# Seven places instead of five for rounded operands, and five steps ahead instead of three, in two of four matrix products

## The chip, the cores and the metric

The kernel runs on one core of one Trainium2 chip. The metric is the device time of one execution in microseconds (us), lower is better. TensorE (PE, with its weight loads PEld) multiplies, VectorE (DVE) and ScalarE (ACT) work element by element, GpSimd (POOL) does little here, and SyncE (SP) issues nearly all DMAs from one queue, in order. Each engine runs its own instructions in the order in which they stand in the program, and waits for the others by semaphores.

## The reference, cut to what matters

An attention with 32 memory slots per head, and behind it two feed-forward blocks:

```
x = attention(q, k, v, phi)            # 4608 tokens x 512
g = relu(x @ w_in1) ** 2               # 512 -> 2048
y = g @ w_out1                         # 2048 -> 512
g = silu(y @ w_in2)                    # 512 -> 2048
out = g @ w_out2                       # 2048 -> 512
```

## The kernel before, in words

There are four matrix products in a row. The first (attention and w_in1) fills the time up to about 337 us. The function `second` computes the second product (w_out1, 337 to 700 us) and, called once more, the last one (w_out2, from about 1049 us to the end). The third product (w_in2) lies between them.

**What `second` does.** The tokens are cut into 6 batches of 768. A batch is computed by a seven-product scheme for 2x2 blocks: instead of eight block products there are seven, named after their right-hand operands B11, B21, T2, T1, T3, B22, T4 (`PRODUCTS`), in this order. B11 to B22 are the loaded blocks (tiles `r`, from `g` in memory), T1 to T4 are sums of them that DVE makes in place (T1 = B12 - B11, T2 = B22 - T1, T3 = B22 - B12, T4 = B21 - T2; lines 758 to 767). In the second product only, ACT first squares each loaded block (line 746).

**A step.** Each of the seven products is done in four steps, one for each quarter h of the inner dimension, so a batch has 28 steps and `second` 168. For a step two things must be ready: its weights (`ws`, on chip), and its operand in two parts, a rounded one and the rest: ACT rounds the operand into the first half of a tile `c` (line 770), and DVE writes what the rounding lost into the second half (line 771). PE then does 12 matmuls of 128x128 by 128x384 (line 799): for each of two weight tiles and two output halves rounded times rounded, rounded times rest, rest times rounded. The first of each three needs only ACT's half, the second needs DVE's.

**What `combos` issues.** One call makes the operand of one step: the squares (for the first step of each pair of blocks), the sums, and the two halves of `c`. The calls run ahead of PE by `AHEAD` steps in the program:

```
for k in range(AHEAD):
    ahead(k)
for k, (b, n, h) in enumerate(steps):
    ahead(k + AHEAD)
```

At the first step of a batch `ahead` also issues the 16 loads of that batch's blocks. A load waits until DVE no longer needs what lies in its place.

**The places.** The tiles `c` come from the pool `s` under the tag "g", which has a fixed number of places. A new `c` needs a place whose former tile has been read for the last time: for another `c` that is PE's last matmul on it. The third product uses the same tag for its output tiles (`g2t`, two for each pair of weight tiles), which leave their place when their DMA to memory has landed. The pools of `second` lie on chip where those of the first product lay.

**What sets the order.** The program is written step by step, but a scheduler then orders each engine's instructions by an estimate of its own of when each can run. The order in which the code emits them decides between those that are ready.

Of the kernel before, what the change touches and what calls it, by code (L numbers as in the profile page):

```python
# [76 lines left out]
def attention_moe_moe(ctx: ExitStack, tc, q, kv, phi, w_in1, w_out1, w_in2, w_out2, out):  # L77
# [577 lines left out]

    pools = [tc.tile_pool(name=n, bufs=k, reuse_waits="tile") for n, k in (("wk", 1), ("wl", 1), ("xa", 1), ("xb", 1), ("s", 5), ("u", 2))]
    wk, wl, xa, xb, spool, upool = (ctx.enter_context(p) for p in pools)
    psum = ctx.enter_context(tc.tile_pool(name="ps", bufs=1, space=PSUM, reuse_waits="tile"))  # L660
    W.update({q: (wk if q < WR + 2 else wl).tile([P, SLOTS, 2, 2 * P], F32R, tag=f"w{q}", name=f"ws{q}") for q in range(WR, NQ)})
# [40 lines left out]
    QS = 2  # L702
    NH = NQ // QS
    HQ = NQ // 2
    AHEAD = 3

    NAMES = ("B11", "B21", "B12", "B22", "T2")
    FREED = ("B11", "T2", "B12", "B22", "B21")
# [4 lines left out]
    def second(src, order, square, to, weights, begin, tiles=tuple(range(10))):  # L713
# [61 lines left out]
        def ahead(k):  # L775
            if k < len(steps):
                b, n, h = steps[k]
                if n == h == 0 and b:
                    quarters(b)
                combos(b, n, h)  # L780

        start = len(begun)
        begin(quarters)
# [4 lines that stand above are left out]
            bank = PRODUCTS[n][1]  # L788
# [221 lines left out]
```

## Time and profile before

| | |
|---|---|
| median of 3 runs | 1420.09 us (1415.77 to 1420.38) |
| the profiled execution | 1416.34 us |
| its span, first to last instruction | 1414.6 us |
| PE busy | 1375.0 us, 97% |
| PEld, DVE, ACT busy | 1311.8, 965.9, 790.7 us |
| DMA queue of SP | 386.62 MB, 80.4% of 16 engines |

The profile is one execution. "Busy" is the time in which an engine executes; what stands behind "<-" names whoever ended a wait. PE's matmuls overlap, so that one takes some 335 ns while the next starts about 174 ns after it. How many start in a stretch is therefore the better measure of PE's pace.

### The profile page before, as it was taken

The numbers are of one execution on the slowest core, as the hardware profiler recorded it, in microseconds if no ns is written. First come the engines' busy times: TensorE is split into PE (matmuls) and PEld (weight loads), VectorE is DVE, ScalarE is ACT, GpSimd is POOL, SyncE is SP. The second block draws the span as 40 slices with busy tenths as digits, with TensorE's granted clock in tenths as the row PEclk, the third lists the DMA queues.
The fourth block names the chain that finished last, engine by engine and source line by source line (L and its number), as shares of the span: only waits on it lengthen the run. The fifth ranks groups of instructions, "written<-read, shape, count | busy, mean of one in ns | idle before, by whom it ended". The sixth has DMA issues, their size and how long they took to land.

```text
span 1414.6 us, 25254 instructions
## 1 busy us (share of the span) xinstructions
PE 1375.0 (97%) x9266; PEld 1311.8 (93%) x9266; DVE 965.9 (68%) x1578; ACT 790.7 (56%) x1305; POOL 22.3 (2%) x44
## 2 busy tenths in 40 slices
PE   6999999999999999999999999999999999999999
PEld 4777877889899999999999999999998999999998
DVE  4666766764697878879756656565438858678583
ACT  3656666676668677685546455454434444444443
POOL 0000000000000000000000000000000000000000
PEclk9999999999999999999999999999999999999999
DMA  9979999899778878789997877879998576665750
GB/s 316 338 250 325 320 335 302 270 340 385 229 240 301 272 265 293 241 296 317 371 312 250 317 274 263 310 251 308 364 400 304 160 244 196 215 218 162 236 153 34
DMA packets 208444, 388.24 MB, mean 274 GB/s; under 512 B 19264, under 2 KB 90944, under 8 KB 208320
## 3 DMA queue, kind: packets, MB, share of 16 engines
q1 hardware_dynamic: 208320, 386.62, 80.4%
q8 instruction: 73, 1.20, 0.3%
q14 instruction: 51, 0.42, 0.1%
HBM read 253.38 MB, written 133.17 MB: 273 GB/s over the span
## 4 chain that ended last, share of the span: by engine, by line
PE 61%; DMA 5%; DVE 3%; ACT 1%; issue 1%; SPq 0%; DVEq 0%; ACTq 0%
PE psa L799 22%; PE psa L918 13%; PE psc L799 12%; PE psc L918 6%; PE psb L799 4%; PE psb L918 3%; DMA r<-g 2%; DVE c L771 1%; DMA ws<-w2o 1%; DMA g<-g2t 1%; DMA st<-moe_w_in 1%; ACT c L770 1%; ACT r L746 1%; DVE r L764 0%; DVE r L767 0%
## 5 line engine op out<-in xcount | busy, mean ns | idle before, releaser
L771 DVE TENSOR_TENSOR c<-r,c 128x768 fp32r<-128x768 f32 x336 | 318.1, 956 | 171.4 <-ACT c L770 171.1
L799 PE MATMUL psa<-c,ws 128*128 128x384 f32 x2304 | 416.0, 337 | 9.9 <-DVE c L771 6.1
L799 PEld LDWEIGHTS psa<-c,ws 128*128 128x128 f32 x2304 | 403.4, 189 | 13.8 <-DVE c L771 8.8
L770 ACT CAST c<-r 128x768 fp32r<-128x768 f32 x336 | 278.4, 835 | 222.9 <-PE psa L799 112.4
L918 PE MATMUL psa<-xc,ws 128*128 128x384 f32 x1152 | 218.0, 336 | 0.0
L613 PEld LDWEIGHTS h<-at,wp 128*128 128x128 f32 x1344 | 180.6, 188 | 36.4 <-ACT gt L622 21.4
L799 PE MATMUL psc<-c,ws 128*128 128x384 f32 x1152 | 206.5, 335 | 2.8 <-ACT c L770 2.8
L799 PEld LDWEIGHTS psc<-c,ws 128*128 128x128 f32 x1152 | 201.0, 188 | 3.2 <-ACT c L770 3.2
L613 PE MATMUL h<-at,wp 128*128 128x288 f32 x1344 | 196.2, 300 | 7.1 <-ACT gt L622 7.1
L918 PEld LDWEIGHTS psa<-xc,ws 128*128 128x128 f32 x1152 | 202.4, 188 | 0.0
L918 PE MATMUL psc<-xc,ws 128*128 128x384 f32 x576 | 110.9, 335 | 0.0
L799 PE MATMUL psb<-c,ws 128*128 128x384 f32 x576 | 106.3, 339 | 1.0 <-DVE c L771 1.0
L799 PEld LDWEIGHTS psb<-c,ws 128*128 128x128 f32 x576 | 101.3, 189 | 2.5 <-DVE c L771 2.4
L918 PEld LDWEIGHTS psc<-xc,ws 128*128 128x128 f32 x576 | 101.2, 188 | 0.0
L622 ACT ACTIVATE gt<-h 128x576 f32<-128x576 f32 x112 | 72.2, 648 | 42.5 <-PE h L613 38.4
L746 ACT ACTIVATE r<-r 128x768 f32<-128x768 f32 x96 | 80.0, 845 | 28.0 <-DMA r<-g 26.3
L206 DVE TENSOR_TENSOR pp<-pw,pp 128x256 f32<-128x256 f32 x148 | 61.3, 420 | 50.0 <-ACT pp L205 48.5
L205 ACT CAST pp<-pw 128x256 fp32r<-128x256 f32 x148 | 58.7, 403 | 55.4 <-DMA w2o<-pp 24.1
L162 ACT CAST top<-st 128x256 f16<-128x256 bf16 (+1 forms) x112 | 57.8, 527 | 31.0 <-DMA st<-moe_w_out 16.7
L932 ACT ACTIVATE g2t<-g2t 128x1152 f32<-128x1152 f32 x48 | 55.1, 1165 | 28.9 <-DVE g2t L683 28.7
L166 DVE SCALAR_TENSOR_TENSOR pw<-st,top 128x256 int32<-128x256 int32 x96 | 41.0, 430 | 36.4 <-ACT top L162 35.4
L685 ACT COPY u<-psa 128x384 f32<-128x384 f32 x72 | 33.9, 475 | 48.0 <-PE psa L918 20.4
(99 smaller groups left out, 1174.6 us busy)
## 6 DMA issues: line engine op xcount, KB each, us to landing
r<-g SPq DMA_DIRECT2D x192, 384.0 KB, 5.0
g<-g2t SPq DMA_DIRECT2D x48, 768.0 KB, 7.1
ws<-w2i SPq DMA_DIRECT2D x136, 256.0 KB, 5.2
ws<-w2o SPq DMA_DIRECT2D x136, 256.0 KB, 3.5
ws<-w1o SPq DMA_DIRECT2D x116, 256.0 KB, 4.5
g<-gt SPq DMA_DIRECT2D x64, 384.0 KB, 5.6
kv<-kv SPq DMA_DIRECT2D x32, 516.0 KB, 6.4
st<-moe_w_out SPq DMA_DIRECT2D x64, 256.0 KB, 5.1
```

The lines of the kernel that those rows point to most:

```text
L162: ins = nc.scalar.copy(top.bitcast(F16).rearrange("p (n h) -> p n h", h=2)[:, :, 1], flat.bitcast(BF16).rearrange("p (n h) -> p n h", h=4) ...
L166: to_f32.last = nc.vector.scalar_tensor_tensor(f.bitcast(I32), flat.rearrange("p (n w) -> p n w", w=2)[:, :n, 1], 13, top, op0=ALU.logical ...
L205: held(nc.scalar.copy(hi, w[:, of]))
L206: tt(lo, w[:, of], hi.bitcast(F32), op=ALU.subtract)
L613: mm = nc.tensor.matmul(h[:, half, :HALF], wp[b, j][:, g, s, fo:fo + P], attnT[b][:, x, g, tk], start=(k == 0), stop=(k == len(ops) - 1),)
L622: nc.scalar.activation(gt[:, f % 2].rearrange("p (h t) -> p h t", h=2), h[:, :, :HALF], AF.Relu)
L746: nc.scalar.activation(raw[b, name, h], raw[b, name, h], AF.Square)
L770: nc.scalar.copy(c[:, 0], r(name))
L771: tt(c[:, 1], r(name), c[:, 0].bitcast(F32), op=ALU.subtract)
L799: mm = nc.tensor.matmul(ps[o][bank], W[h * QS + u][:, slot(n), wi, o * P:(o + 1) * P], x[:, xi, u], start=(n in FIRST and h == u == m == 0 ...
L918: mm = nc.tensor.matmul(ps[q][bank], W[q][:, slot(n), wi, k * P:(k + 1) * P], x[:, xi, k], start=(n in FIRST and k == 0 and m == 0), stop= ...
L932: nc.scalar.activation(gq[q][:, :3], gq[q][:, :3], AF.Silu)
```

## The change

The pool of the rounded operands gets seven places instead of five, and `second` issues the operands five steps ahead instead of three. Nothing is added or removed: DVE has 1578 instructions in both programs, ACT 1305, and SP issues 1204 DMAs.

```diff
-    pools = [tc.tile_pool(name=n, bufs=k, reuse_waits="tile") for n, k in (("wk", 1), ("wl", 1), ("xa", 1), ("xb", 1), ("s", 5), ("u", 2))]
+    pools = [tc.tile_pool(name=n, bufs=k, reuse_waits="tile") for n, k in (("wk", 1), ("wl", 1), ("xa", 1), ("xb", 1), ("s", 7), ("u", 2))]
...
-    AHEAD = 3
+    AHEAD = 5
```

Since both numbers go into the scheduler, the order on the engines changes. On DVE in the second product, second batch, these rows stood from the rest of B21's first quarter (c_4965) to that of its fourth (c_5020); r_5040 and r_5041 are T2, and pp belongs to the preparation of the next weights:

```order
L771 TENSOR_TENSOR c_4965<-r_4863,c_4965 128x768
L758 TENSOR_TENSOR r_4858<-r_4870,r_4858 128x768
L771 TENSOR_TENSOR c_4982<-r_4863,c_4982 128x768
L762 TENSOR_TENSOR r_5041<-r_4876,r_4858 128x768
L764 TENSOR_TENSOR r_4870<-r_4876,r_4870 128x768
L771 TENSOR_TENSOR c_4999<-r_4864,c_4999 128x768
L206 TENSOR_TENSOR pp_7600<-pw_7555,pp_7600 128x256
L206 TENSOR_TENSOR pp_7604<-pw_7555,pp_7604 128x256
L767 TENSOR_TENSOR r_4863<-r_4863,r_5040 128x768
L762 TENSOR_TENSOR r_5041<-r_4876,r_4858 128x768
L771 TENSOR_TENSOR c_5020<-r_4864,c_5020 128x768
```

Now the same four (c_4931 to c_4992) stand as follows; T2 is r_5008 and r_5009:

```order
L771 TENSOR_TENSOR c_4931<-r_4833,c_4931 128x768
L758 TENSOR_TENSOR r_4828<-r_4840,r_4828 128x768
L215 TENSOR_TENSOR pw_7555<-pw_7555 128x256
L758 TENSOR_TENSOR r_4828<-r_4840,r_4828 128x768
L771 TENSOR_TENSOR c_4956<-r_4833,c_4956 128x768
L767 TENSOR_TENSOR r_4833<-r_4833,r_5008 128x768
L771 TENSOR_TENSOR c_4975<-r_4834,c_4975 128x768
L762 TENSOR_TENSOR r_5009<-r_4846,r_4828 128x768
L764 TENSOR_TENSOR r_4840<-r_4846,r_4840 128x768
L216 TENSOR_TENSOR pw_7555<-pw_7555 128x256
L771 TENSOR_TENSOR c_4992<-r_4834,c_4992 128x768
```

The four have moved ahead of work that isn't theirs: from the last rest of the batch before (T4, fourth quarter) to that of B21's fourth quarter DVE had 31 instructions, 20 of them of 128x768, and has 26 now, 19 of them of 128x768.

On ACT, where the third product ends and the last one begins, these rows stood (c_11525 to c_11534 are the four quarters of B11, c_11551 and c_11566 the first two of B21; g2t is the third product's output):

```order
L770 CAST c_11525<-r_11453 128x768
L932 ACTIVATE g2t_10935<-g2t_10935 128x1152
L932 ACTIVATE g2t_10936<-g2t_10936 128x1152
L770 CAST c_11528<-r_11453 128x768
L934 ACTIVATE g2t_10935<-psa_10937 128x384
L770 CAST c_11531<-r_11454 128x768
L770 CAST c_11534<-r_11454 128x768
L770 CAST c_11551<-r_11459 128x768
L770 CAST c_11566<-r_11459 128x768
```

Now there are (c_11537, c_11540 and c_11557 are the first three quarters of B21):

```order
L770 CAST c_11525<-r_11453 128x768
L690 COPY u2_10985<-psa_10937 128x384
L770 CAST c_11528<-r_11453 128x768
L690 COPY u2_10987<-psa_10944 128x384
L770 CAST c_11531<-r_11454 128x768
L932 ACTIVATE g2t_10935<-g2t_10935 128x1152
L932 ACTIVATE g2t_10936<-g2t_10936 128x1152
L770 CAST c_11534<-r_11454 128x768
L770 CAST c_11537<-r_11459 128x768
L770 CAST c_11540<-r_11459 128x768
L770 CAST c_11557<-r_11460 128x768
L934 ACTIVATE g2t_10935<-psa_10937 128x384
L685 COPY u1_11606<-psa_11543 128x384
```

Three roundings now stand ahead of the third product's last activations, where there was one. Behind this piece, and behind a copy of PE's sums of B11 (u1, L685), comes the rounding of B21's fourth quarter. On DVE its rest and T2's first quarter stand there now, at the start of the last product, as follows (c_11572 and c_11591):

```order
L771 TENSOR_TENSOR c_11572<-r_11460,c_11572 128x768
L758 TENSOR_TENSOR r_11453<-r_11489,r_11453 128x768 x2
L758 TENSOR_TENSOR r_11454<-r_11490,r_11454 128x768 x2
L762 TENSOR_TENSOR r_11588<-r_11495,r_11453 128x768
L764 TENSOR_TENSOR r_11489<-r_11495,r_11489 128x768
L767 TENSOR_TENSOR r_11459<-r_11459,r_11588 128x768
L762 TENSOR_TENSOR r_11588<-r_11495,r_11453 128x768
L764 TENSOR_TENSOR r_11489<-r_11495,r_11489 128x768
L771 TENSOR_TENSOR c_11591<-r_11588,c_11591 128x768
```

All the sums of T1 stand behind B21's last rest now; before, they were mixed in between the rests of B21, and 5 instructions stood between the last of these and T2's first. At the start of the second product nothing has moved: DVE's first 38 instructions there stand in the same order in both programs.

## Rows read from the trace of the kernel before

**Rows 1.** The page's first part: busy time, share of the span, instructions.
```profile
PE 1375.0 (97%) x9266; PEld 1311.8 (93%) x9266; DVE 965.9 (68%) x1578; ACT 790.7 (56%) x1305; POOL 22.3 (2%) x44
```

**Rows 2.** Stretches of the span: busy time and instructions by engine, clock, DMA.
```profile
337.00:400.00 63.00, 59.02 (x325) 57.66 (x326) 46.40 (x61) 46.28 (x68) 0.00 (x0) 0.97 0.79 266
400.00:460.00 60.00, 58.70 (x334) 57.86 (x333) 51.65 (x75) 42.52 (x69) 0.00 (x0) 1.00 0.83 280
460.00:520.00 60.00, 60.00 (x347) 60.00 (x346) 48.41 (x72) 43.43 (x70) 0.00 (x0) 1.00 0.79 263
520.00:580.00 60.00, 58.79 (x333) 57.49 (x332) 51.26 (x75) 41.80 (x68) 0.00 (x0) 1.00 0.85 282
...
640.00:700.00 60.00, 59.35 (x341) 59.03 (x340) 54.38 (x78) 33.14 (x53) 0.00 (x0) 1.00 0.97 343
700.00:1049.00 349.00, 349.00 (x2004) 349.00 (x2004) 197.03 (x369) 174.94 (x317) 0.00 (x0) 1.00 0.87 303
1049.00:1080.00 31.00, 25.55 (x131) 23.95 (x131) 22.59 (x28) 13.02 (x18) 0.00 (x0) 0.94 0.93 350
1080.00:1414.00 334.00, 331.07 (x1901) 330.75 (x1900) 232.71 (x275) 150.21 (x202) 0.00 (x0) 1.00 0.58 186
```

**Rows 3.** PE's waits, 400 to 700 us: total, times, longest.
```profile
PE psa L799 <- DVE c L771: 2.1, 3, 0.9
PE psb L799 <- DVE c L771: 1.0, 2, 0.7
```

**Rows 4.** Waits of all engines, 364 to 396 us.
```profile
DVE c L771 <- ACT c L770: 14.2, 11, 3.3
ACT r L746 <- DMA r<-g: 7.3, 6, 3.9
```

**Rows 5.** Stretches in the second product's first and second batch, columns as in rows 2.
```profile
346.00:366.00 20.00, 16.73 (x85) 15.70 (x84) 19.73 (x25) 11.55 (x17) 0.00 (x0) 0.91 0.70 237
366.00:396.00 30.00, 30.00 (x175) 30.00 (x174) 15.84 (x22) 25.69 (x40) 0.00 (x0) 1.00 0.82 258
396.00:421.00 25.00, 23.73 (x134) 22.90 (x132) 25.00 (x37) 14.02 (x24) 0.00 (x0) 1.00 0.72 236
```

**Rows 6.** Groups of instructions by line: busy us, mean ns, then idle before.
```profile
L770 ACT CAST c<-r 128x768 fp32r<-128x768 f32 x336 | 278.4, 835 | 222.9 <-PE psa L799 112.4 <-PE psc L799 49.7 <-PE psb L799 39.2
L746 ACT ACTIVATE r<-r 128x768 f32<-128x768 f32 x96 | 80.0, 845 | 28.0 <-DMA r<-g 26.3 <-DVE pw L166 0.8 <-DVE pp L206 0.4
```

**Rows 7.** PE's waits, 1040 to 1090 us.
```profile
PE psa L799 <- DVE c L771: 3.2, 2, 2.8
PE psa L799 <- ACT c L770: 2.3, 3, 1.0
```

**Rows 8.** ACT in order of time, 1041 to 1062 us: start, length, instruction, wait.
```profile
1056.01 1.56 ACT L770 CAST c<-r 128x768 fp32r<-128x768 f32 x2 [1.25 <-PE psa L799]
...
1059.94 1.57 ACT L770 CAST c<-r 128x768 fp32r<-128x768 f32 x2 [2.37 <-PE psa L799]
```

**Rows 9.** PE in order of time, 1047 to 1086 us.
```profile
1049.34 2.27 PE L799 MATMUL psa<-c,ws 128*128 128x384 f32 x12
...
1073.12 3.11 PE L799 MATMUL psa<-c,ws 128*128 128x384 f32 x12 [2.79 <-DVE c L771]
...
1085.22 1.04 PE L799 MATMUL psc<-c,ws 128*128 128x384 f32 x5
```

**Rows 10.** DVE in order of time, 1044 to 1082 us.
```profile
1072.11 0.95 DVE L771 TENSOR_TENSOR c<-r,c 128x768 fp32r<-128x768 f32 x1
...
1079.93 1.82 DVE L771 TENSOR_TENSOR c<-r,c 128x768 fp32r<-128x768 f32 x2
```

**Rows 11.** The stretch behind PE's longest wait there, columns as in rows 2.
```profile
1074.50:1077.90 3.40, 3.40 (x12) 3.40 (x11) 3.40 (x5) 1.29 (x2) 0.00 (x0) 0.50 0.22 33
```

**Rows 12.** ACT and DVE in order of time, around 393 to 400 us.
```profile
393.28 0.85 ACT L746 ACTIVATE r<-r 128x768 f32<-128x768 f32 x1 [0.34 <-DMA r<-g]
...
399.77 0.95 DVE L758 TENSOR_TENSOR r<-r 128x768 f32<-128x768 f32 x1
```

## The prediction

> **What bounds the kernel now.** I read the page's first part first: PE is busy 97% of the span, no other engine above 68% [rows 1]. So only stretches in which PE falls short can give time back. The windows show them [rows 2]. I take counts of matmuls rather than busy time, since a busy PE need not be at its pace. In 460 to 520 us PE never stops and does 347 matmuls in 60 us (0.173 us each), in the third product 2004 in 349 us (0.174). I take 0.1735 us, or 346 in 60 us; a step of 12 is 2.08 us. By this pace the losses are:
>
> - 337 to 400 us: 325 instead of 363, 38 x 0.1735 = 6.6 us (first batch of the second product).
> - 400 to 460, 520 to 580 and 640 to 700 us: 334, 333 and 341 instead of 346, 30 x 0.1735 = 5.2 us. Each holds a batch's passage from B21 to T2.
> - 1049 to 1080 us: 131 instead of 179, 48 x 0.1735 = 8.3 us (start of the last product).
> - 460 to 520 us, the third product and the last product's rest: nothing that can be told from the pace.
>
> Together 20.1 us. Who ends the waits: after 400 us DVE with the rests [rows 3]; at the last product's start DVE with the rests (3.2 us, one wait of 2.8) and ACT with the roundings (2.3 us) [rows 7].
>
> **Why PE waits at T2.** In 366 to 396 us DVE is busy 15.84 of 30 us, then 25.00 of 25 us in 396 to 421 [rows 5]: first it waits 14.2 us for roundings [rows 4], then the sums for T2 and T1 come at once and it runs late. What it lacks is a lead, worked up while it idled. The lead is limited by places: ACT's roundings wait longest for PE, 222.9, 112.4 and 39.2 + 49.7 us by PE's three banks [rows 6].
>
> **Stage one of the change, the second product's later batches.** Two more places and two more steps let the operands stand two steps further ahead, 2 x 2.08 = 4.2 us. The largest single loss is 13 x 0.1735 = 2.3 us. Besides, DVE's order changes: from the old batch's last rest to B21's last rest there are 26 instructions instead of 31, one less of 128x768. One of those starts 0.87 us after the other (0.95 long, 1.82 for two) [rows 10], so work that is not this batch's is put behind it. I take all of the 5.2 us as gone. Bounds: with the pace of 347 per 60 us the loss is 33 x 0.173 = 5.7 us; PE's plain waits for DVE are only 2.1 + 1.0 = 3.1 us [rows 3]. So 3.1 to 5.7.
>
> **Stage two, the last product's start.** Four of the five places hold the third product's outputs, so the first roundings pass through the fifth one after another: ACT waits 1.25 and 2.37 us for PE's matmuls on the rounding before [rows 8], and PE waits in its turn. With seven places three are free, and three roundings stand ahead of the old activations in ACT's order. From 1049.34 us PE does 96 matmuls up to T2 (12 of them the third product's), in the order of both programs, and 54 up to the end of B11. Unstalled, B11 ends at 1049.34 + 54 x 0.1735 = 1058.7 and T2 is reached at 1066.0 us; its first two matmuls (0.6 us with their tail) need no rest, so from 1066.6 on PE waits. Before it waited from 1073.12 - 2.79 = 1070.3 on [rows 9], 3.7 us later.
>
> But then comes the next wait. In the new ACT order the rounding of B21's last quarter stands behind two copies of B11's sums (0.48 each), so it ends at about 1059.7, and its rest on DVE at 1060.6. Behind that stand nine sums and T2's rest, ten times 0.87 = 8.7: T2's rest is ready at 1069.3. Before it was ready at 1072.11 + 0.95 = 1073.06 [rows 10], 3.8 us later. So PE waits 2.7 us, as long as before (2.8). What follows is paced by DVE with the same instructions, some in another order; the passage that PE reached at 1085.22 [rows 9] I expect at 1081.8: a gain of 3.4 us.
>
> PE's clock belongs to this. In the 3.4 us behind the long wait the granted clock is 0.50, the 1.2 GHz level, and PE does 12 matmuls where its pace gives 19.6: 7.6 x 0.1735 = 1.3 us [rows 11]. As the wait stays, I leave this loss in; if it goes too, the gain is 4.7. If the T2 wait grows by all that is won before it, the gain is 0. So 0 to 4.7, and 3.4 taken. The Trainium skill, "TensorE: Matmul & The Clock Gate", Part 1, says that the throttled state is the default and activity releases it; by this rule a T2 wait that shrank would give the 1.3 us back too (-9.9 instead of -8.6 in the sum below), and the trace agrees in so far as the drop stands behind the wait.
>
> **What I cost at nothing.** The first batch of the second product: DVE is busy 19.73 of 20 us in 346 to 366 [rows 5] and its first 38 instructions stand in the same order, so 6.6 us stay. The third product has no loss [rows 2], so more places for its outputs give nothing. The last product behind 1080 us likewise. The pool is 12 KB per partition larger and lies over the first product's places: between 0 and one wait for a transfer, longest 3.9 us [rows 4]; I take 0. The 16 loads of a batch are issued two steps earlier in the program on SP; they still wait for DVE's last use of their place, and the weights queued behind them are used some 12 steps later (25 us, the cover): 0, or again 3.9 once if that cover were gone.
>
> **The sum.** -5.2 - 3.4 = -8.6 us. The profiled execution took 1416.34 us (span 1414.6 and 1.7 around it), so 1407.7, a factor of 0.9939. The median of the runs is 3.75 us above the profiled one; the same factor gives 1420.09 x 0.9939 = 1411.5 us.
>
> **Rivals.**
>
> 1. *The lead in the second product is not set by places.* Then the change doesn't do there what it says. For it: in 364 to 396 us no wait of ACT for PE is among the long ones; ACT waits 7.3 us for loads before its squares [rows 4] and is busy 25.69 of 30 us [rows 5]. Squares and roundings in ACT's order may set the lead. Against it: the roundings now stand earlier in that order. Only stage two's gain: 1416.34 - 3.4 = 1412.9, median 1416.7.
> 2. *The T2 wait eats the gain at the last product.* For it: the chain of DVE there has no gap. Only the 5.2: 1411.1, median 1414.9.
> 3. *All waits are lack of space.* With it all 20.1 us would go: 1396.2, median 1400. Against it stands the first batch, where DVE itself has no time left [rows 5]. The Trainium skill, "Perfetto Trace Analysis", section "Identifying Performance Opportunities", says that a gap that repeats on the engine that should be saturated can mean too little memory for the next tile; by this rule the same would follow. The trace bears it out at the last product's start alone.
> 4. *Nothing that can be measured:* both stages find other limits, 1420.
> 5. *Slower: squares come late.* ACT is 86% busy in 366 to 396 us [rows 5], and two more roundings (2 x 0.835 us [rows 6]) stand ahead of squares. The last square starts at 393.28 and ends at 394.13; the first sum that needs it starts at 399.77 [rows 12], a margin of 5.6 us. Beyond this, the sum waits, and as DVE is in order all rests queued behind it, then PE. Two roundings take 1.7 us of the margin, so it holds unless loads add 3.9 us. To be slower by over 0.3% it must cost 8.6 + 4.3 = 12.9 us in five batches, 2.6 each: squares 8.2 us later than now.
>
> **How the numbers follow.** About 0.3%, or 4.3 us, is what a measurement of this kernel can tell from no change. Both stages as summed 0.60 (likeliest range 3.1 + 3.4 to 5.7 + 4.7, median 1409.7 to 1413.6); rival 1 0.15; rival 2 0.10; rival 3 0.03; rival 4 0.07; rival 5 0.05. Faster by over 0.3% (below 1415.8): the sum, rival 3, over half of rival 2, a fifth of rival 1, 0.71. Slower: 0.06. Else 0.23. The prediction is 1411.5 us, that of the likeliest case. The range goes from 1405 (a gain of both stages at its bound, and the runs' own spread of over 4 us) to 1418 (rival 1 with a little added); what lies outside is rival 3, 4 for the most part, and 5.
>
> **What the new profile would show.** Right: 345 to 347 matmuls in 400 to 460, 520 to 580 and 640 to 700 us, shifted a little, and no waits of PE for DVE there; at the last product's start no wait of ACT or PE for each other up to T2, T2's rest near 1069 us less what was won before it, a wait of about 2.7 us there, and the clock at 0.50 behind it; the first batch as it was, with 6.6 us lost. Wrong: PE still waits for rests at T2 in the second, fourth and sixth batch (then the lead isn't the places'); DVE waits for squares there (rival 5); or the T2 wait of the last product is 5 us or more (rival 2).

## The result, and the profile after

With the change the kernel takes 1407.07 us (median of 6 runs, 1405.54 to 1411.67), before 1420.24 us (6 runs): a ratio of 0.9919, 95% interval 0.9901 to 0.9937. The forecast was 1411.5 us. Timed once more beside other kernels it took 1410.12 us, 0.9944 (0.9924 to 0.9963). The two intervals overlap, and the ratio that the forecast used, 0.9939, lies in the second and just above the first.

The profiled execution took 1405.59 us with a span of 1403.8. These are its stretches, to be held against [rows 2] (columns: window; then length, busy time and instructions of PE, PEld, DVE, ACT, POOL; granted clock; DMA share; GB/s):

```profile
337.00:400.00 63.00, 59.90 (x333) 59.25 (x334) 48.95 (x63) 47.31 (x70) 0.00 (x0) 0.97 0.78 267
400.00:460.00 60.00, 60.00 (x346) 60.00 (x345) 52.79 (x77) 44.43 (x72) 0.00 (x0) 1.00 0.81 279
460.00:520.00 60.00, 60.00 (x347) 60.00 (x346) 51.14 (x75) 42.98 (x70) 0.00 (x0) 1.00 0.83 287
520.00:580.00 60.00, 60.00 (x346) 60.00 (x346) 52.67 (x77) 44.02 (x71) 0.00 (x0) 1.00 0.83 285
580.00:640.00 60.00, 60.00 (x347) 60.00 (x346) 50.79 (x74) 42.80 (x68) 0.00 (x0) 1.00 0.83 287
640.00:700.00 60.00, 60.00 (x346) 60.00 (x346) 45.97 (x69) 29.64 (x50) 0.00 (x0) 1.00 0.95 332
```

The three short counts, 334, 333 and 341, are 346 now: PE has no gap from 400 us to the end of the second product. At 337 to 400 us it still falls short, with 333 instead of 363. The last product starts some 7 us earlier than before, and at its start one wait of PE is left of the five in [rows 7]:

```profile
PE psa L799 <- DVE c L771: 2.9, 1, 2.9
```

On PE's own timeline it stands behind T2's first two matmuls, as before [rows 9]:

```profile
1058.95 0.56 PE L799 MATMUL psa<-c,ws 128*128 128x384 f32 x2
1062.37 3.88 PE L799 MATMUL psa<-c,ws 128*128 128x384 f32 x12 [2.86 <-DVE c L771]
...
1074.47 8.16 PE L799 MATMUL psc<-c,ws 128*128 128x384 f32 x46
```

The last row is the passage that stood at 1085.22 [rows 9], 10.75 us earlier. The next view is DVE's timeline there: the rest of B21's last quarter, then nine sums without a gap, then T2's rest (L771).

```profile
1052.67 0.96 DVE L771 TENSOR_TENSOR c<-r,c 128x768 fp32r<-128x768 f32 x1 [1.24 <-ACT c L770]
1053.55 3.56 DVE L758 TENSOR_TENSOR r<-r 128x768 f32<-128x768 f32 x4
1057.03 0.95 DVE L762 TENSOR_TENSOR r<-r 128x768 f32<-128x768 f32 x1
1057.89 0.95 DVE L764 TENSOR_TENSOR r<-r 128x768 f32<-128x768 f32 x1
1058.76 0.95 DVE L767 TENSOR_TENSOR r<-r 128x768 f32<-128x768 f32 x1
1059.63 0.95 DVE L762 TENSOR_TENSOR r<-r 128x768 f32<-128x768 f32 x1
1060.50 0.95 DVE L764 TENSOR_TENSOR r<-r 128x768 f32<-128x768 f32 x1
1061.37 0.95 DVE L771 TENSOR_TENSOR c<-r,c 128x768 fp32r<-128x768 f32 x1
```

From 1052.67 to 1061.37 it is 8.70 us, the ten times 0.87 of the prediction. Behind PE's wait the clock falls, as in [rows 11]; the row covers the 3.4 us from the end of the wait:

```profile
1062.30:1065.70 3.40, 3.33 (x11) 3.32 (x12) 3.40 (x5) 0.83 (x1) 0.00 (x0) 0.57 1.06 403
```

To compare kernels whose products start at different times, I count matmuls from the second product's first one on (6048 in the last three products) and take, for a stretch of them, the time from the start of its first to the start of the next stretch's first, less 0.1735 us for each. That is the loss against PE's pace, in us. A stretch without any wait shows 0.2 for 336 matmuls, since the pace is a shade under 0.1742.

| kernel | second product starts | its first batch (336) | its five others (1680) | last product's start (numbers 4000 to 4400) | span |
|---|---|---|---|---|---|
| before | 337.34 | 6.42 | 6.47 | 8.62 | 1414.6 |
| before, again | 337.67 | 6.33 | 6.27 | 8.63 | 1414.6 |
| the change | 335.87 | 6.16 | 1.12 | 4.99 | 1403.8 |
| the change, again | 338.65 | 7.69 | 1.12 | 4.85 | 1409.3 |
| seven places, three steps ahead | 337.14 | 7.60 | 1.12 | 5.20 | 1407.1 |
| six places, three steps ahead | 337.59 | 6.14 | 1.25 | 5.93 | 1406.5 |
| sums late, five places | 340.19 | 1.18 | 1.13 | 4.65 | 1404.0 |
| sums late, seven places | 340.81 | 2.74 | 1.13 | 0.95 | 1401.4 |
| sums late in first batches | 337.24 | 2.75 | 1.15 | 0.94 | 1397.7 |
| sums behind all of T2's rests | 336.31 | 7.96 | 1.12 | 2.59 | 1403.7 |

The long wait in the second product's first batch, which the change leaves, looks like this on PE and on ACT (the kernel with the change):

```profile
358.71 0.62 PE L799 MATMUL psc<-c,ws 128*128 128x384 f32 x2 [2.78 <-ACT c L770]
...
357.10 3.77 ACT L770 CAST c<-r 128x768 fp32r<-128x768 f32 x5 [0.96 <-DVE r L762]
```

The two matmuls are T1's first, which stand on PE ahead of most of T2's second quarter. T1's rounding is the second of ACT's five, behind that of T2's last quarter, and this one waits for the sum on DVE (L762). Ahead of that sum DVE has made four of T3's and T4's sums, and six of them stand ahead of T2's second rest.

In the first pair of profiles the 10.8 us of span are thus 5.35 in the five later batches, 3.63 at the last product's start, 0.26 in the first batch, and 1.47 that were won before the second product began.

### The profile page after: what moved, and what is told of

It is laid out like the page before. It is cut to its first block, busy times and chain, and to the rows that moved or that the text cites. A ratio compares the mean times of both kernels' runs of the same rounds, so it can differ in the third digit from the quotient of the medians.

```text
span 1403.8 us, 25185 instructions
## 1 busy us (share of the span) xinstructions
PE 1370.3 (98%) x9266; PEld 1312.0 (93%) x9266; DVE 966.1 (69%) x1578; ACT 790.3 (56%) x1305; POOL 22.2 (2%) x44
## 4 chain that ended last, share of the span: by engine, by line
PE 86%; DMA 8%; DVE 3%; ACT 1%; SPq 1%; issue 1%; POOL 0%; ACTq 0%; DVEq 0%; POOLq 0%
PE psa L799 28%; PE psc L799 14%; PE psa L918 13%; PE h L613 8%; PE psc L918 7%; PE psb L799 6%; PE psb L918 3%; DMA st<-moe_w_out 2%; PE pswp L426 2%; DMA r<-g 1%; PE h L590 1%; PE pskv L385 1%; DMA g<-gt 1%; DMA kv<-kv 1%; DMA ws<-w2o 1%
## 5 line engine op out<-in xcount | busy, mean ns | idle before, releaser
L771 DVE TENSOR_TENSOR c<-r,c 128x768 fp32r<-128x768 f32 x336 | 315.5, 953 | 157.4 <-ACT c L770 156.0
L799 PE MATMUL psa<-c,ws 128*128 128x384 f32 x2304 | 412.4, 338 | 5.0 <-DVE c L771 3.6
L799 PEld LDWEIGHTS psa<-c,ws 128*128 128x128 f32 x2304 | 404.5, 189 | 6.3 <-DVE c L771 4.5
L799 PE MATMUL psc<-c,ws 128*128 128x384 f32 x1152 | 204.9, 336 | 2.8 <-ACT c L770 2.8
L799 PEld LDWEIGHTS psc<-c,ws 128*128 128x128 f32 x1152 | 200.9, 188 | 3.1 <-ACT c L770 3.1
L799 PE MATMUL psb<-c,ws 128*128 128x384 f32 x576 | 102.8, 336 | 0.0
L799 PEld LDWEIGHTS psb<-c,ws 128*128 128x128 f32 x576 | 100.8, 188 | 0.0
L206 DVE TENSOR_TENSOR pp<-pw,pp 128x256 f32<-128x256 f32 x148 | 62.0, 423 | 51.0 <-ACT pp L205 49.7
L685 ACT COPY u<-psa 128x384 f32<-128x384 f32 x72 | 34.1, 476 | 49.5 <-PE psa L918 20.2
```

Source lines behind the costliest of these rows:

```text
L206: tt(lo, w[:, of], hi.bitcast(F32), op=ALU.subtract)
L771: tt(c[:, 1], r(name), c[:, 0].bitcast(F32), op=ALU.subtract)
L799: mm = nc.tensor.matmul(ps[o][bank], W[h * QS + u][:, slot(n), wi, o * P:(o + 1) * P], x[:, xi, u], start=(n in FIRST and h == u == m == 0 ...
```

## The experiments

My theory was that the waits are a missing lead of DVE over PE, that the places set this lead, and that the T2 waits which stay in the two first batches come from sums that stand ahead of T2's rests on DVE. The rivals: the number of steps ahead sets the lead; the order of the sums alone is the cause; DVE has too much to do in the first batches whatever its order. In the first four runs the kernel before took 1419.55 us (12 runs), in the last four 1418.12 us (11 runs).

**Seven places, three steps ahead.** One of the two edits alone:

```diff
-    pools = [... ("s", 5) ...]
+    pools = [... ("s", 7) ...]
...
     AHEAD = 3
```

> Seven places, issued three steps ahead as before. Theory (places): the lead is set by the places alone; how far the program issues ahead is only a tie-break of the scheduler, and the order on DVE and PE is that of the change, on ACT but for one swap. So 0.992 of the time before (some 1408 us), 345 to 347 matmuls in 400-460, 520-580 and 640-700 us, and a T2 wait of some 3.4 us at the last product's start, 0.5 more than with the change since the swap puts a copy ahead of B21's last rounding. Rival (steps ahead): the program's three steps cap the lead; as before in the second product, and at most the 3.4 us of the last product's start are won: 0.9975 or 1.0.

1409.03 us, 0.9923 (0.9898 to 0.9949): as the change. The order of instructions explains why: with seven places PE's and DVE's orders are the same at three and at five steps ahead, and on ACT one rounding stands behind a copy instead of ahead of it. The windows of the second product:

```profile
400.00:460.00 60.00, 60.00 (x347) 60.00 (x346) 52.81 (x77) 43.09 (x69) 0.00 (x0) 1.00 0.80 277
520.00:580.00 60.00, 60.00 (x346) 60.00 (x345) 53.22 (x78) 44.22 (x72) 0.00 (x0) 1.00 0.84 287
640.00:700.00 60.00, 60.00 (x346) 60.00 (x345) 49.62 (x74) 30.00 (x50) 0.00 (x0) 1.00 0.96 336
```

The full counts are there without the two steps. So with seven places the second half of the change does nothing that can be measured: the scheduler reaches the same order on PE and DVE without it. Five steps with five places were not run. At T2 in the last product PE waits 0.16 us for ACT and 2.87 for DVE, 3.0 together, where 3.4 were expected. The swap on ACT costs 5.20 - 4.99 = 0.2 us at the last product's start, less than the 0.5 expected.

**Six places, three steps ahead.** The same with `("s", 6)`.

> Six places, three steps ahead: one place more than before. Theory (places): one step of lead, 2.08 us, against a largest loss of 2.3 us, so the second product's later batches lose at most 1 us of the 5.2; at the last product's start two places are free instead of one, and about half of the 3.4 us is won: -4.2 - 1.7 = -5.9 us, 0.996. Rival (steps ahead): nothing, 1.0. Rival (a threshold, only the seventh place counts): 1.0 too, but with the lead of DVE at T2 unchanged.

1411.71 us, 0.9943 (0.9922 to 0.9964). In the second product one more place takes nearly all (6.47 to 1.25, where 1.12 is none), at the last product's start most: PE waits 0.8 us for ACT there, where it was 2.3 with five places [rows 7]. That is 5.22 and 2.69 us won, where 4.2 and 1.7 were expected.

```profile
PE psa L799 <- DVE c L771: 2.8, 1, 2.8
PE psa L799 <- ACT c L770: 0.8, 1, 0.8
```

The lead, from the end of a rest on DVE to the start of PE's first matmul on it, goes up to 6.3 us with five places late in the last product, to 8.4 with six and to 10.5 with seven: one step of 2.1 us for each place, with three steps ahead as with five. That shows the places to be the limit of the lead there. In the second product, where squares stand in ACT's order too, the lead is shorter but grows as well: in the kernels with their sums as they were, its median over the second half of a batch, from the second batch on, is 2.6 to 5.1 us with five places, 4.1 to 6.3 with six and 5.3 to 8.7 with seven. Together with the waits that went, this refutes rival 1 of the prediction. Nor do the places work by moving sums out of the way: of the eight sums of T3 and T4 in the second, fourth and sixth batch, 6 to 8 stand ahead of T2's four rests on DVE in the kernel before and in the change alike.

**Late sums, five places and three steps ahead.** DVE makes a sum of T3 only behind the rest of the same quarter of T1, and one of T4 only behind that of T3 (`follow` fixes the order of two instructions of an engine). Here the kernel before is what is edited:

```diff
-            elif name == "T1":
-                tt(r("B12"), r("B22"), r("B12"), op=ALU.subtract)
-                raw[b, "T3", h] = r("B12")
-            elif name == "T3":
-                tt(r("B21"), r("B21"), r("T2"), op=ALU.subtract)
-                raw[b, "T4", h] = r("B21")
             c = cc[b, n, h] = spool.tile([P, 2, QS, TH], F32R, tag="g", name="c")
             nc.scalar.copy(c[:, 0], r(name))
-            tt(c[:, 1], r(name), c[:, 0].bitcast(F32), op=ALU.subtract)
+            rest = tt(c[:, 1], r(name), c[:, 0].bitcast(F32), op=ALU.subtract)
+            if name == "T1":
+                t = tt(r("B12"), r("B22"), r("B12"), op=ALU.subtract)
+                raw[b, "T3", h] = r("B12")
+            elif name == "T3":
+                t = tt(r("B21"), r("B21"), r("T2"), op=ALU.subtract)
+                raw[b, "T4", h] = r("B21")
+            if name in ("T1", "T3"):
+                follow(t, rest)
```

> Five places and three steps ahead as before, but DVE may make the sums of T3 only behind the rest of the same quarter of T1, and those of T4 only behind that of T3. Theory (places): the missing lead remains: in the second product's second, fourth and sixth batch the waits shrink by the sums that stood ahead of T2's rest (up to half of the 5.2 us stays), while the T2 waits of both first batches shrink, by 3 to 5 us each with the clock: -2.6 - 4 - 4 = some -10 us, 0.993. Rival (order): the sums ahead of T2's rests are the whole cause, the lead is not needed: the later batches reach 346 matmuls in 60 us too: -13 us, 0.991. Second rival: sums made late delay the rests of T3 and T4, and the waits only move: 1.0.

1405.51 us, 0.9897 (0.9875 to 0.9919). Here my theory falls short and the rival of order holds: the later batches have no wait at all (1.13), at a lead that still goes no further than 6.3 us. None of the eight sums of T3 and T4 stands ahead of T2's rests now.

```profile
400.00:460.00 60.00, 60.00 (x347) 60.00 (x346) 51.37 (x77) 44.80 (x72) 0.00 (x0) 1.00 0.79 273
520.00:580.00 60.00, 60.00 (x347) 60.00 (x346) 53.57 (x79) 44.03 (x71) 0.00 (x0) 1.00 0.83 288
640.00:700.00 60.00, 60.00 (x347) 60.00 (x346) 48.78 (x72) 31.27 (x51) 0.00 (x0) 1.00 0.95 329
```

So the waits there were a burst of sums against a lead that was too short for it; a longer lead and a smaller burst each remove them whole, and together they give no more (1.13 below). The first batch too loses its waits at T1 and T2 (6.42 to 1.18). At the last product's start 4.65 of 8.62 stay: PE waits for ACT as before, 2.3 us, for want of places.

**Late sums, seven places.** The same edit on the changed kernel.

> The change, and the sums of T3 and T4 behind the rests as in the run before. Theory: the waits that the change left, 3 us at T2 in each first batch and the low clock behind them (some 1.5 us each), come from sums that stand ahead of T2's rests on DVE; without them the rest of T2's first quarter in the last product comes 3 x 0.87 = 2.6 us earlier, in the second product that of T2's second quarter over 3 us: -4 and -5 us beyond the change, 0.986 of before. Rival (DVE simply has too much to do in the first batch): the wait moves to T1 or T3, nothing or under 2 us beyond the change, 0.991.

1401.33 us, 0.9870 (0.9846 to 0.9894). At the last product's start 0.95 us are left. PE's timeline there, with T2's first two matmuls in the first row (L801 is L799 of the kernel before, L765 its L771):

```profile
1060.57 0.56 PE L801 MATMUL psa<-c,ws 128*128 128x384 f32 x2
1061.51 6.37 PE L801 MATMUL psa<-c,ws 128*128 128x384 f32 x35 [0.38 <-DVE c L765]
```

The wait of 2.86 us is 0.38, and 35 matmuls take 6.37 us at the full clock behind it, where 12 took 3.88. The two edits add up at this place: 3.63 by the places alone, 3.97 by the sums alone, 7.67 by both. The first batch loses 2.74 us, 3.4 less than in the change's first profile and 5.0 less than in its second, where the clock falls at the batch's start as it does here (last section); 5 were expected.

**Late sums in the first batches only.** The same code, with the order fixed for `b == 0` alone; in the later batches the sums stand behind the rests in the code but the scheduler is free, so that their order is close to, not exactly, that of the change: there 5 to 8 of the eight sums stand ahead of T2's rests, in the change 6 to 8.

> The change, with the sums of T3 and T4 spread behind the rests in the two first batches alone; the later batches are ordered as in the change. Theory: in the later batches seven places leave no wait, so late sums have nothing to give there, and this is as fast as with late sums in all batches: 0.987 of before. Rival: late sums in the later batches gave part of the gain: 0.990.

1399.52 us, 0.9871 (0.9852 to 0.9889): as with the order fixed in all batches (0.9870). Its median is the lowest of the kernels, but the two were timed against different runs of the kernel before, and their ratios do not differ. The stretches of the two first batches, to be held against 325 and 131 in [rows 2]:

```profile
337.00:400.00 63.00, 62.39 (x346) 61.82 (x347) 53.55 (x68) 49.78 (x74) 0.00 (x0) 0.97 0.84 296
...
1049.00:1080.00 31.00, 30.62 (x176) 30.20 (x175) 29.61 (x36) 16.33 (x23) 0.00 (x0) 1.00 1.00 363
```

**All sums in one piece behind T2's rests.** On the changed kernel, in all batches:

```diff
+        rest = {}
...
-                tt(r("B12"), r("B22"), r("B12"), op=ALU.subtract)
+                follow(tt(r("B12"), r("B22"), r("B12"), op=ALU.subtract), rest[b, "T2"])
...
-                tt(r("B21"), r("B21"), r("T2"), op=ALU.subtract)
+                follow(tt(r("B21"), r("B21"), r("T2"), op=ALU.subtract), rest[b, "T2"])
...
-            tt(c[:, 1], r(name), c[:, 0].bitcast(F32), op=ALU.subtract)
+            rest[b, name] = tt(c[:, 1], r(name), c[:, 0].bitcast(F32), op=ALU.subtract)
```

> The change, with all eight sums of T3 and T4 behind the last rest of T2, in one piece ahead of T1's rests, instead of one by one behind the rests of T1 and T3. Theory: T2's rests come in time in both first batches, but T1's first rest comes 8 x 0.87 = 7.0 us later than with the sums spread, where it was 0.7 and 3.7 us ahead of PE: PE waits about 6 us at T1 in the second product's first batch and about 3 us in the last product's, and the clock falls behind both waits; no waits in later batches, where the lead is 5 us or more. Some 11 us over the kernel with the sums spread: 0.994 to 0.996 of before. Rival (the order within the first batch makes no difference as DVE has the same work): 0.987, as with the sums spread.

1408.16 us, 0.9930 (0.9911 to 0.9949), no better than the change. DVE's timeline in the second product's first batch shows T2's last two rests, eight sums, and only then T1's rests (L772 is L771 before); below it PE's (L800), from T1's first two matmuls on:

```profile
358.54 2.00 DVE L772 TENSOR_TENSOR c<-r,c 128x768 fp32r<-128x768 f32 x2
360.46 3.56 DVE L765 TENSOR_TENSOR r<-r 128x768 f32<-128x768 f32 x4
363.93 3.56 DVE L768 TENSOR_TENSOR r<-r 128x768 f32<-128x768 f32 x4
367.41 5.29 DVE L772 TENSOR_TENSOR c<-r,c 128x768 fp32r<-128x768 f32 x6
```

```profile
362.08 0.52 PE L800 MATMUL psc<-c,ws 128*128 128x384 f32 x2
362.44 2.91 PE L800 MATMUL psa<-c,ws 128*128 128x384 f32 x12
368.42 3.86 PE L800 MATMUL psc<-c,ws 128*128 128x384 f32 x13 [3.07 <-DVE c L772]
```

The rest comes 7 us later, and PE waits for it, in the place and for the reason expected. My size was wrong: 3.1 us instead of 6 (and 1.3 instead of 3 at the last product's start), since I had forgotten the 12 matmuls of T2 (2.91 us) that stand on PE between T1's first two and its third. The clock was expected to fall behind both waits; it fell behind the first (granted 0.57 from 368.40 to 371.80 us) and not behind the second (1.00 from 1074.60 to 1078.00). The rival, that the order within the first batch is indifferent, falls.

**Before and the change, profiled again.** No edit in either.

> The kernel before, unchanged, profiled once more. Theory: the 1.9 us by which the changed kernel's second product starts earlier is scatter of the first product, in which no engine's order differs: here the second product starts anywhere from 335 to 341 us (337.3 in the first profile), while the losses behind it are as before within 0.5 us: 6.4 in the first batch, 5.4 more than pace in the five others, 8.6 at the last product's start. Rival: the larger pool lets the second product's first operands in earlier, then it starts at 337.3 again.

> The change, unchanged, timed and profiled again. Theory: the second product starts anywhere from 335 to 341 us, and from there to the end it takes as long as in the first profile within 1.5 us; 0.9925 to 0.994 of before, since 5.3 + 3.6 us are the change's. Rival (first product gains too): starts at 335.4 again, and 0.992 or less.

Before: 1416.39 us in its one run, start of the second product at 337.67. The change: 1410.12 us, 0.9944 (0.9924 to 0.9963), start at 338.65 instead of 335.87. So the 1.47 us of the first pair are no effect of the change: over the ten profiles the second product starts anywhere between 335.87 and 340.81 us, with no connection to places or sums that shows. (The kernel before alone would not have told: it started at 337.34 and 337.67.) The losses in the later batches and at the last product's start repeat within 0.2 us; the first batch's does not (below). And at the third product's start PE waited once, 1.02 us at 706.85 us, for a copy on ACT that waited for a transfer; the first profile has no such wait. The larger pool need not be its cause: late sums with five places have one like it, 0.61 us at 701.42 us, for the same copy and the same kind of transfer. So the time from the second product's start to the end was 2.7 us longer (1409.3 - 338.65 against 1403.8 - 335.87): 1.53 in the first batch and some 1.3 there, more than the 1.5 that I had expected.

## Why the prediction was right, step by step

- **Second product's later batches, -5.2 us.** Measured 6.47 - 1.12 = 5.35 us. The place and the sum are right. The reason given, "what it lacks is a lead", is half of it: the late sums show that without one more place another order removes the same waits.
- **ACT's waits for PE.** The row was misread: the 222.9 us in [rows 6] are all the idle time before the roundings, and PE's three banks ended 112.4, 49.7 and 39.2 of it, 201.3 together. That most of it is PE's, as the argument needs, stays true.
- **"Two more places and two more steps".** With seven places the steps did nothing; the places alone did it. The prediction did not part the two, though DVE's order for seven places and three steps would have shown it beforehand.
- **Last product's start, -3.4 us.** Measured 8.62 - 4.99 = 3.63. The chain that was to replace the old one came as worked out: T2's rest 8.70 us behind B21's last, a wait of 2.86 us (2.7 forecast, 2.79 before), the low clock behind it, and the passage at 1085.22 earlier by 10.75, of which 10.75 - 1.47 - 0.26 - 5.35 = 3.67 us were won here. One step of the chain came out by luck. The prediction put two copies of B11's sums ahead of B21's last rounding and left out the 0.83 us of the rounding itself; in fact one copy stands ahead of it, and begins before B11's last matmul has ended:

```profile
1051.28 0.48 ACT L685 COPY u<-psa 128x384 f32<-128x384 f32 x1 [0.59 <-PE psa L799]
1051.81 0.83 ACT L770 CAST c<-r 128x768 fp32r<-128x768 f32 x1
```

The rounding ends 10.41 us behind the matmul at 1042.23 that stood at 1049.34 before, where 1059.7 - 1049.34 = 10.4 was forecast. And ACT does still wait for PE ahead of it, 0.69 and 1.24 us, which the prediction ruled out; PE does not wait for ACT.
- **First batch, 0.** Measured 0.26 less in one profile and 1.3 more in the other; the wait of 2.8 us is the same in all four profiles of the two kernels. What differs is the clock at the batch's start (last section).
- **The rest at nothing.** In the first profile PE waits neither in the third product nor in the last behind its start, and no wait of PE for a transfer came with the larger pool. In the repeated profile there is one, through a copy on ACT, of 1.02 us, and a kernel with five places shows the like.
- **The sum.** -8.6 forecast; the two terms together are 8.98 by the traces. The profiled execution won 10.75, and the medians 13.2 (first timing) or 8.0 (second). What lies beyond 9 us in the profiled pair is for the most part the first product's scatter, 1.47 us. In the medians of the first timing, 4 us beyond the traces, its share is not shown: only one run of each kernel was profiled there.
- **Rivals.** The lead does follow the places (6.3, 8.4, 10.5 us), and the waits of the later batches went, so rival 1 falls. The T2 wait did not grow (2.86 us), so rival 2 does. Rival 3, that all waits are lack of space, fails as expected: in the second product's first batch it is the order of sums on DVE, and with that mended the long wait goes at five places; at the last product's start it is both. My ground against it, "DVE itself has no time left", was wrong too: DVE was busy 19.73 of 20 us [rows 5], but partly with sums that could wait. Rival 4, nothing that can be measured, falls with both timings (0.9919 and 0.9944, neither interval reaching 1). Late squares (rival 5) held up nothing: behind 366 us DVE never waits for a square in the second product.

## What to carry to other kernels

A busy feeder says nothing about what it is busy with: before giving it a deeper buffer, look at which instructions stand ahead of the one that is waited for, and whether they are needed so early. Here a deeper buffer cost 12 KB per partition and removed 9 us, and a different place for sums cost nothing and removed 14.6 (by the table 6.42 + 6.47 + 8.62 less 1.18 + 1.13 + 4.65); both together gave 0.987. Where a scheduler orders the instructions, a parameter of the code's own order may be dead: compare the orders with each parameter alone before putting a price on it.

## What the runs showed of the hardware that I had not expected

The second product begins with two short waits of PE, 1.46 us in all profiles and some 0.37. In five of the ten profiles the clock falls behind them and in the others not, so one program can show either, as the change's own two profiles do. All five are among the six with seven places, and none of the four with five or six places shows it; whether the places have a part in it these few profiles cannot tell. This is the change, in the repeated profile and then in the first, over the same work:

```profile
340.60:344.00 3.40, 3.40 (x13) 3.40 (x12) 3.40 (x5) 3.35 (x6) 0.00 (x0) 0.50 1.05 404
```

```profile
337.80:341.20 3.40, 3.40 (x22) 3.40 (x21) 3.40 (x5) 3.31 (x6) 0.00 (x0) 1.00 0.99 355
```

At 0.50, the 1.2 GHz level, a matmul starts every 0.32 us there instead of every 0.174, ten of them in a row, which costs some 1.5 us. That is the whole difference between the first batch's 6.16 and 7.69 us in the table, and also why the fastest kernel shows 2.75 there and late sums with five places 1.18.
